# A new written-out order of instructions on all five queues of a fused linear-attention and feed-forward kernel

## The chip, the core and the metric

The kernel runs on one core of one Trainium2 chip. The core has a tensor engine (PE, TensorE), a vector engine (DVE), a scalar engine (ACT, ScalarE), GpSimd (POOL) and a sync engine (SP, SyncE) that mostly issues DMAs. Each engine works through its own list of instructions in order and waits on semaphores for the others. The metric is the device time of one execution, in microseconds (us).

## What is computed

Four batches, eight heads, 768 positions, head size 64. Block by block along the sequence, a decaying causal attention without softmax keeps a 64x64 state per head; its output x (3072 tokens x 512) goes through a feed-forward layer of width 2048 with the activation h + sin(alpha h)^2 / alpha.

```python
for b in range(nb):
    intra = np.einsum('bhic,bhjc->bhij', qb, kb) * Dmask[None]
    intra = np.einsum('bhij,bhjd->bhid', intra, vb)
    inter = np.einsum('bhid,bhde->bhie', qb * lam_pow[None], kv_state)
    out[:, :, sl] = intra + inter
    kv_state = lam_block[None, :, None, None] * kv_state + np.einsum('bhsd,bhse->bhde', kb_dec, vb)
...
h = x @ w_in
s = np.sin(alpha * h)
g = h + s * s / (alpha + 1e-09)
return (g @ w_out).astype(np.float32)
```

Inputs are float32; matmuls are in bfloat16 with float32 sums.

## The kernel before

**Attention in quads.** The attention is cut into 24 "quads" t = 0 to 23 (`quad0`, L758, for t below 8; `quad`, L959, for the others). For one quad: `ks`, `qs` multiply k and q by powers of lam and make them bfloat16 (L789 or L985; with .0 and .1 for halves), `vs` copies v to bfloat16 (L801, L804, L996). For t below 8, `Tk` and `Tq` transpose k and q on TensorE (L819) and `cT` copies the result out of PSUM (L825, L831); for t from 8 a DMA transposes (`DT`, L1008). `S` is the product of k and q (L850, L1021), `mask` the causal mask on it (L855, L1033, DVE), `Z` the state's increment (L867, L1072), `Zi` its copy for the second half of the quad (L886), `I` the part of the output from the state (L897, L1041), `O` the part from S and v (L912, L1061), `x` the copy of the result into the tile xT, which feeds the feed-forward part (L929, L1113); `Zs` (L952, L1136) and `Z` with a digit (L940, L1130) bring the state up to date. From t = 8 the S of the next quad stands in the same instruction group as O.

**Feed-forward in chunks.** Six chunks c of 512 tokens. `A c.m` (`grp_A`, L1146) makes 128 of the 2048 columns of h: 4 matmuls of 512 columns (L1160) into one of six PSUM banks. In chunk 0 some are made in halves of 256 tokens (h0, h1), two m at a time, as 8 matmuls of half width; a part of them with the first 2 or 3 of the 4 slices of x is a group of its own, marked e. Then `sin` (L1172, ACT), `sq`, the square (L1179 on ACT, L1180 on POOL or DVE) and `g` (L1184, DVE), which frees the bank. `B c.s.m` (`grp_B`, L1224) is 4 matmuls of the second product (L1237) for 128 tokens s and a quarter m of the 2048; after m = 3 the result is copied out (`o`, L1253) and stored (`st`, L1256). The last tile (`last_tile`, L1195) is made in three cuts (L1205, L1213, L1216).

**Loads.** The first eight quads' k, q, v come by `load_quad` (L746, tags `quad k0.1` and the like: the first digit counts pairs of heads, the second the half of the 256 rows of sequence; some loads take two pairs at once, 256 KB, others one, 128 KB). Quad 0 needs the pairs 0 and 1 with .0, quad 1 the pairs 2 and 3 with .0, quads 2 and 3 the same pairs with .1; quads 4 to 7 the numbers 4 to 7. One load, k1.0, is issued by ACT, the others by SyncE. The later quads' loads come by `load_half` (L635). The weights come in blocks w0, w0b (256 KB each in bfloat16), w1 to w7 (512 KB) through POOL's queue (`w_block`, L655). Small constants (`consts`, L675) are tagged c0 to c30: c12, c13 are the decay tables Lk, Lq of the quads 0 to 7, c15, c16 those of the others, c10 the logarithm of lam, c28 the loading of the sine table.

**What sets the order.** Every operation is recorded with the buffers that it reads and writes (`Program.add`, L220). `schedule` (L267) then lays the operations on the five engines. Where the table `ORDER` in `TUNE` gives a list for an engine, that list alone is the engine's order; dependencies become semaphore waits (`emit`, L458). What is left to `schedule`: which PSUM bank a group gets, and how many matmuls on zeros (`zero_mms`, L617, L619) stand in a gap that it expects on TensorE in the first 60 us; these fillers keep the engine active and are never read.

The lines that change are the five lists of `ORDER`, L59 to L158.

Of the kernel before, what the change touches and what calls it, by code (L numbers as in the profile page):

```python
# [58 lines left out]
    ORDER={'ACT': ['c0', 'alpha in', 'lam', 'c10', 'alpha', 'c13', 'c12', 'quad k1.0', 'c15', 'cT0.0', 'c16', 'vs1',  # L59
                   'cT1.0', 'x0', 'cT3', 'Zi1.0', 'c28', 'x1', 'Zs0.1', 'Zs1.1', 'Zs1.0', 'sin0.4h0', 'sin0.2h0',  # L60
                   'sin0.5h0', 'sq0.4h0', 'Zi3.0', 'x2', 'sin0.3h0', 'x3', 'sin0.1', 'sin0.4h1', 'sin0.5h1',
                   'sin0.8h1', 'sin0.9h1', 'sin0.8h0', 'sin0.0', 'sin0.9h0', 'sq0.0', 'sin0.6', 'sin0.7', 'sin0.11',
                   'sin0.2h1', 'sq0.11', 'sin0.3h1', 'vs4', 'sin0.13', 'sin0.12', 'sq0.12', 'sin0.14h0', 'sin0.14h1',
                   'sin0.15h0', 'sin0.15h1', 'sq0.14h1', 'cT4.1', 'oh1', 'vs7', 'vs5', 'Zi4.1', 'oh0', 'x4', 'vs6',
                   'Zi5.0', 'sin0.10', 'cT6', 'oh2', 'x5.0', 'Zi6.0', 'Zs4.0', 'Zs3.0', 'oh3', 'cT7', 'Zi7.1',
                   'sin1.1', 'sin1.3', 'sq1.3', 'sin1.0', 'sin1.2', 'sin1.6', 'sin1.4', 'sq1.6', 'sin1.5', 'Zs7.1',
                   'sq1.5', 'Zs7.0', 'sin1.7', 'vs9', 'sin1.9', 'sin1.11', 'sin1.8', 'sq1.8', 'sin1.10', 'sin1.13',
                   'Zs6.1', 'vs8', 'sin1.14', 'sq1.13', 'sin1.15', 'sq1.15', 'sin1.12', 'x8', 'Zs8.1', 'Zs8.0', 'x9',
                   'vs10', 'vs11', 'Zs9.0', 'Zs9.1', 'x10', 'x11', 'st0', 'o4', 'sin2.0', 'o5', 'sin2.3', 'sin2.1',
                   'sin2.4', 'sin2.2', 'st2', 'sin2.5', 'sin2.6', 'o6', 'sin2.8', 'sin2.11', 'sin2.7', 'st3', 'vs15',  # L70
# [12 lines left out]
                   'o22', 'st18', 'st22', 'o21', 'st20', 'st21', 'o23.0', 'st23.0', 'o23.2', 'st23.2'],
           'DVE': ['c24', 'c6', 'c1', 'c2', 'c19', 'c25', 'c8', 'c23', 'c22', 'c9', 'c11', 'qs0', 'c14', 'c18', 'ks3',
                   'vs0', 'ks0', 'qs1.1', 'cT0.1', 'cT1.1', 'Zi0.0', 'Zi0.1', 'c26', 'mask0', 'qs2.0', 'ks2.1',
                   'mask1', 'Zi1.1', 'Z0.0', 'Z0.1', 'cT2', 'c30', 'vs2', 'mask2', 'Zi2.0', 'Zs0.0', 'Zi2.1', 'Z1.1',
                   'mask3', 'Zi3.1', 'g0.5h0', 'g0.4h0', 'Z2.1', 'Z3.0', 'g0.2h0', 'Z3.1', 'cT4.0', 'sq0.4h1',
                   'g0.3h0', 'g0.4h1', 'g0.1', 'g0.5h1', 'g0.8h1', 'g0.0', 'qs5.1', 'g0.9h1', 'g0.8h0', 'g0.9h0',
                   'g0.7', 'g0.11', 'g0.6', 'sq0.13', 'g0.13', 'g0.2h1', 'g0.12', 'g0.3h1', 'g0.14h1', 'g0.15h1',
                   'g0.15h0', 'mask4', 'Zi4.0', 'cT5', 'g0.14h0', 'ks6.1', 'Z4.0', 'qs6.1', 'Z4.1', 'mask5', 'sq0.10',  # L90
                   'Zi5.1', 'g0.10', 'ks7.0', 'x5.1', 'qs7.0', 'Z5.0', 'Zi6.1', 'Zs4.1', 'mask6', 'Z5.1', 'Zs2.0',
                   'Zs5.1', 'x6', 'Z6.0', 'Zs2.1', 'Z6.1', 'Zs3.1', 'mask7', 'Zs5.0', 'Zi7.0', 'Zs6.0', 'o2', 'c21',
                   'x7', 'Z7.0', 'o3', 'Z7.1', 'g1.3', 'o0', 'sq1.0', 'sq1.1', 'g1.0', 'sq1.2', 'g1.1', 'g1.2', 'o1',
                   'g1.6', 'g1.5', 'g1.4', 'sq1.7', 'g1.7', 'g1.9', 'g1.8', 'sq1.10', 'g1.11', 'g1.10', 'g1.13',
# [12 lines left out]
                  'A0.11', 'A0.7', 'A0.2h1', 'B0.0.0', 'A0.13', 'A0.12', 'A0.14h0', 'A0.14h1', 'B0.1.0', 'B0.1.1',
                  'Tk4', 'B0.2.0', 'S4', 'Z4', 'Tk5', 'Tq5', 'B0.0.1', 'I4', 'O4', 'S5', 'Z5', 'A0.10', 'B0.3.0',
                  'Tk6', 'Tq6', 'B0.2.1', 'I5', 'O5', 'S6', 'Z6', 'B0.3.1', 'Tk7', 'Tq7', 'B0.2.2', 'I6', 'O6', 'Z7',
                  'S7', 'B0.1.2', 'B0.3.2', 'B0.2.3', 'B0.3.3', 'I7', 'O7', 'B0.0.2', 'A1.1', 'A1.3', 'A1.0',  # L110
                  'B0.0.3', 'A1.2', 'A1.6', 'A1.4', 'B0.1.3', 'A1.5', 'A1.9', 'A1.7', 'A1.11', 'A1.8', 'A1.10',
                  'A1.13', 'A1.14', 'A1.15', 'B1.0.0', 'B1.0.1', 'S8', 'A1.12', 'B1.0.2', 'O8', 'B1.1.0', 'B1.1.1',
                  'O9', 'B1.1.2', 'B1.0.3', 'O10', 'B1.1.3', 'B1.2.0', 'O11', 'B1.2.1', 'A2.0', 'A2.3', 'A2.1',
                  'A2.4', 'A2.2', 'A2.5', 'A2.6', 'B1.2.2', 'B1.2.3', 'A2.8', 'A2.11', 'A2.7', 'A2.12', 'A2.9',
                  'A2.10', 'B1.3.0', 'B1.3.1', 'B1.3.2', 'A2.13', 'B1.3.3', 'A2.15', 'A2.14', 'B2.0.0', 'O12',
                  'B2.0.1', 'B2.0.2', 'B2.1.0', 'O13', 'B2.1.1', 'B2.1.2', 'B2.2.0', 'O14', 'B2.0.3', 'B2.1.3', 'O15',
                  'B2.2.1', 'A3.1', 'A3.0', 'A3.2', 'A3.4', 'A3.7', 'A3.3', 'B2.2.2', 'A3.10', 'A3.5', 'B2.2.3',
                  'A3.6', 'A3.8', 'O16', 'B2.3.0', 'B2.3.1', 'B2.3.2', 'O17', 'A3.9', 'A3.11', 'A3.14', 'B2.3.3',
                  'A3.12', 'A3.15', 'O18', 'A3.13', 'B3.0.0', 'B3.0.1', 'O19', 'B3.0.2', 'A4.0', 'A4.1', 'B3.1.0',
# [1276 lines left out]
```

## Time and profile before

| what | value |
|---|---|
| runs shown | 215.23, 215.52, 216.65 us; median 215.52 |
| profiled execution | 216.6 us, its span 214.7 us |
| mean granted TensorE clock | 0.991 |
| busy: PE, DVE, ACT, POOL | 206.2, 126.1, 127.1, 125.8 us |
| matmuls on zeros (L619) | 110 of 2185, 9.5 us |
| HBM read, written | 27.27 MB, 6.29 MB |
| q, k, v loads of SyncE to landing, median of each kind | 4.2 to 10.3 us |

How to read the profile: a line of a timeline gives the start and the length in us, the engine, the line of the kernel, the operation, the tiles written and read, their shapes, the number of instructions merged, and in brackets how long the engine sat idle before and what released it. SPq, ACTq are the engines' issuing of DMAs; PEld is TensorE's weight load. A row of the table by stretches gives for each engine its busy time, then the granted TensorE clock, the mean busy share of the 16 DMA engines and GB/s. In the view of DMAs, q1 is SyncE's queue, q0 that of POOL, q10 that of ACT: packets, MB, and time taken as a share of the 16 engines in the stretch asked for; a row of issues gives KB each and the us from issue to landing.

### The profile page before, as it was taken

How to read it: one execution, taken by the hardware profiler on the slowest of the kernel's cores; microseconds unless marked ns; L12 is line 12 of the kernel's file. 1: busy time of each engine (PE TensorE's matmuls, PEld its weight loads, DVE VectorE, ACT ScalarE, POOL GpSimd, SP SyncE). 2: the span in 40 equal slices, each digit the busy share in tenths (PEclk: the TensorE clock that was granted, in tenths of full speed). 3: DMA queues.
4: the chain of work that ended last, by engine and by line, in shares of the span. 5: the costliest groups of instructions: out<-in, count | busy, mean ns of one | idle time of the engine just before them, and what ended most of it. 6: DMA issues, size and time to landing. Idle time of an engine off the chain costs nothing.

```text
span 214.7 us, 5310 instructions
## 1 busy us (share of the span) xinstructions
PE 206.2 (96%) x2185; PEld 110.7 (52%) x2185; DVE 126.1 (59%) x226; ACT 127.1 (59%) x236; POOL 125.8 (59%) x140
## 2 busy tenths in 40 slices
PE   7697899999999999999999999999999999999994
PEld 6684565655444455444455455454454544444454
DVE  4759578899868882454663477733616732463320
ACT  3056678975079955766536974957563726753231
POOL 2753387930328960799996988788765331771400
PEclk9998899999999999999999999999999999999999
DMA  5999999899998887999989999952630011310115
GB/s 154 281 215 226 216 262 267 206 173 185 181 202 163 174 151 164 231 219 223 222 115 228 198 244 172 191 125 84 101 98 0 3 49 52 147 62 35 52 52 194
DMA packets 88666, 33.91 MB, mean 158 GB/s; under 512 B 68402, under 2 KB 85698, under 8 KB 88642
## 3 DMA queue, kind: packets, MB, share of 16 engines
q1 hardware_dynamic: 79984, 23.01, 57.3%
q0 software_dynamic: 4752, 4.19, 12.3%
q10 hardware_dynamic: 3906, 6.37, 8.5%
q8 instruction: 17, 0.28, 0.6%
q14 instruction: 7, 0.06, 0.1%
HBM read 27.27 MB, written 6.29 MB: 156 GB/s over the span
## 4 chain that ended last, share of the span: by engine, by line
PE 87%; DMA 4%; SPq 3%; DVE 3%; ACT 2%; issue 1%; ACTq 0%
PE M_ps L1160 39%; PE M_ps L1237 37%; DMA q<-in_q_dram 4%; SPq L753 3%; PE M_ps L1061 2%; PE M_ps L1205 2%; PE M_ps L1041 2%; PE A_ps L1021 1%; DVE S_m L855 1%; PE M_ps L912 1%; PE M_ps L1072 1%; PE A_ps L850 1%; PE M_ps L819 1%; PE M_ps L867 1%; PE M_ps L897 1%
## 5 line engine op out<-in xcount | busy, mean ns | idle before, releaser
L1180 POOL TENSOR_TENSOR u<-t 128x512 bf16<-128x512 bf16 x73 | 74.6, 1039 | 51.0 <-ACT t L1172 50.1
L1184 DVE SCALAR_TENSOR_TENSOR gT<-u,r_sb,M_ps 128x512 bf16<-128x512 bf16 (+1 forms) x104 | 70.7, 703 | 56.5 <-POOL u L1180 51.7
L1160 PE MATMUL M_ps<-xT,w 128*128 128x512 bf16 (+1 forms) x416 | 90.4, 367 | 0.1
L1237 PE MATMUL M_ps<-w,gT 128*128 128x512 bf16 x368 | 87.8, 380 | 0.0
L1172 ACT ACTIVATE t<-M_ps,alpha_sb 128x512 bf16<-128x512 f32 (+1 forms) x104 | 65.5, 653 | 31.0 <-PE M_ps L1160 30.1
L1160 PEld LDWEIGHTS M_ps<-xT,w 128*128 128x128 bf16 x416 | 40.3, 99 | 43.1 <-DVE gT L1184 1.2
L1237 PEld LDWEIGHTS M_ps<-w,gT 128*128 128x128 bf16 x368 | 34.4, 98 | 39.4 <-DVE Zf L940 0.3
L985 POOL TENSOR_TENSOR qk<-k,Lk 128x512 bf16<-128x512 f32 x16 | 16.6, 1042 | 11.8 <-DMA k<-in_k_dram 11.8
L1113 ACT CAST xT<-M_ps 128x512 bf16<-128x512 f32 x16 | 9.3, 584 | 23.1 <-PE A_ps L1021 19.8
L1033 DVE TENSOR_TENSOR S_m<-A_ps,maskl 128x768 bf16<-128x768 f32 x16 | 15.3, 954 | 6.1 <-PE A_ps L1021 6.0
L985 POOL TENSOR_TENSOR qk<-q,Lq 128x512 bf16<-128x512 f32 x16 | 16.6, 1039 | 2.2 <-DMA q<-in_q_dram 1.8
L1253 ACT COPY osb<-M_ps 128x512 f32<-128x512 f32 x19 | 11.0, 585 | 10.5 <-PE M_ps L1237 10.3
L619 PE MATMUL M_ps<-zeros 128*128 128x128 bf16 (+1 forms) x110 | 9.5, 252 | 1.5 <-DVE zeros L679 1.5
L1136 ACT CAST Zq<-Zf 64x256 bf16<-64x256 f32 x24 | 9.7, 403 | 1.8 <-DVE Zf L1130 1.2
L855 DVE TENSOR_TENSOR S_m<-A_ps,maskq 128x1024 bf16<-128x1024 f32 x8 | 9.8, 1222 | 1.5 <-PE A_ps L850 1.4
L996 ACT CAST v<-v 128x512 bf16<-128x512 f32 x16 | 9.6, 618 | 1.1 <-DMA v<-in_v_dram 1.1
L619 PEld LDWEIGHTS M_ps<-zeros 128*128 128x128 bf16 x110 | 8.0, 114 | 1.7 <-DVE zeros L679 1.5
L789 POOL TENSOR_TENSOR qk<-q,Lq 128x256 bf16<-128x256 f32 (+1 forms) x7 | 5.2, 740 | 5.0 <-DVE qk L789 4.4
L819 PE MATMUL M_ps<-ident,qk 128*128 128x128 bf16 x64 | 5.2, 220 | 2.8 <-POOL qk L789 2.8
L1179 ACT ACTIVATE u<-t 128x512 bf16<-128x512 bf16 x11 | 6.9, 629 | 0.4
L1130 DVE TENSOR_TENSOR Zf<-M_ps,Zf 128x256 f32<-128x256 f32 x10 | 4.2, 418 | 4.3 <-ACT xT L1113 4.3
L789 POOL TENSOR_TENSOR qk<-k,Lk 128x512 bf16<-128x512 f32 (+1 forms) x6 | 4.9, 832 | 3.1 <-DMA k<-in_k_dram 2.5
(83 smaller groups left out, 136.5 us busy)
## 6 DMA issues: line engine op xcount, KB each, us to landing
q<-in_q_dram SPq DMA_DIRECT2D x23, 256.0 KB, 4.8
out_dram<-osb ACTq DMA_DIRECT2D x23, 256.0 KB, 2.3
v<-in_v_dram SPq DMA_DIRECT2D x38, 128.0 KB, 4.2
k<-in_k_dram SPq DMA_DIRECT2D x37, 128.0 KB, 4.6
w<-in_moe_w_out_dram POOLq DMA_DIRECT2D x4, 512.0 KB, 9.5
w<-in_moe_w_in_dram POOLq DMA_DIRECT2D x3, 512.0 KB, 11.3
k<-in_k_dram SPq DMA_DIRECT2D x5, 256.0 KB, 8.7
v<-in_v_dram SPq DMA_DIRECT2D x5, 256.0 KB, 10.3
```

The costliest lines, as they stand in the source:

```text
L619: last = e.matmul(m_ps[i][:, 0:c], zeros[:, 0:128], zeros[:, 0:c])
L789: rec(en, lambda e, L=L, gs=slice(g0, g0 + n): e.tensor_tensor(o[:, :, gs], i[:, :, gs], L, ALU.mult), *(((0.65, 0.58) if en == "DVE" else ...
L855: rec("DVE", lambda e: e.tensor_tensor(S_m[jm][:, :, :].rearrange("p (h a b) c -> p h a (b c)", h=2, a=2), Av().rearrange("p h (a x) -> p ...
L985: rec(en, lambda e, L=L, gs=slice(g0, g0 + m): e.tensor_tensor(o[:, :, gs], i[:, :, gs], L, ALU.mult), *(((0.65, 0.58) if en == "DVE" else ...
L1033: rec("DVE", lambda e: e.tensor_tensor(S_m[jm][:, :, :].rearrange("p (a b) c -> p a (b c)", a=4)[:, :, 0:192], A_ps[:, :, :].rearrange("p ...
L1136: rec(en, lambda e, rows=rows, en=en: (e.copy if en == "ACT" else e.tensor_copy)(Zq[jj][rows, :, rows], Zf[jj][rows, :, :].rearrange("p i ...
L1160: last = e.matmul(m_ps[vb.i][:, N * i:N * i + N], w1[:, kc, 128 * mm:128 * (mm + 1)], xT[x][:, kc, ts], start=(kc == 0 and i == 0), stop=( ...
L1172: rec("ACT", lambda e, i=i, mm=mm: e.activation(t16[tt][:, N * i:N * i + N], m_ps[vb.i][:, N * i:N * i + N], ACTF.Sin, scale=alpha_sb[:, m ...
L1180: return e.tensor_tensor(u16[tt][:, :], t16[tt][:, :], t16[tt][:, :], ALU.mult)
L1184: rec("DVE", lambda e, i=i, mm=mm: e.scalar_tensor_tensor(out=gT[g][:, mm, ts], in0=u16[tt][:, N * i:N * i + N], scalar=r_sb[:, mm:mm + 1] ...
L1237: last = e.matmul(m_ps[vb.i], gT[g][:, m, 128 * s4:128 * (s4 + 1)], w2[:, m, :], start=(m == 0 or (split and m == 8)), stop=(m == NM - 1 o ...
L1253: rec("ACT", lambda e: e.copy(osb[o][:, :], m_ps[vb.i]), 0.585, 0.48, reads=[vb.key], writes=[f"o.{o}"], frees=[vb], tag=f"o{gsi}")
```

## The change

All five lists of `ORDER` are replaced; nothing else in the file is touched. Each list has the same entries as before in another order: the search for the order was made anew with a set of delays in which every load lands late at random. The beginnings of the lists, which cover the first four quads:

```diff
-    ORDER={'ACT': ['c0', 'alpha in', 'lam', 'c10', 'alpha', 'c13', 'c12', 'quad k1.0', 'c15', 'cT0.0', 'c16', 'vs1',
-                   'cT1.0', 'x0', 'cT3', 'Zi1.0', 'c28', 'x1', 'Zs0.1', 'Zs1.1', 'Zs1.0', 'sin0.4h0', 'sin0.2h0',
+    ORDER={'ACT': ['lam', 'c0', 'c10', 'c16', 'alpha in', 'c12', 'c15', 'c13', 'quad k1.0', 'cT0.0', 'alpha', 'vs1',
+                   'Zi1.0', 'cT1.0', 'c28', 'x0', 'x1', 'cT3', 'Zs1.1', 'Zs0.1', 'Zs1.0', 'sin0.2h0', 'Zi3.0', 'x2',
...
-           'DVE': ['c24', 'c6', 'c1', 'c2', 'c19', 'c25', 'c8', 'c23', 'c22', 'c9', 'c11', 'qs0', 'c14', 'c18', 'ks3',
-                   'vs0', 'ks0', 'qs1.1', 'cT0.1', 'cT1.1', 'Zi0.0', 'Zi0.1', 'c26', 'mask0', 'qs2.0', 'ks2.1',
-                   'mask1', 'Zi1.1', 'Z0.0', 'Z0.1', 'cT2', 'c30', 'vs2', 'mask2', 'Zi2.0', 'Zs0.0', 'Zi2.1', 'Z1.1',
-                   'mask3', 'Zi3.1', 'g0.5h0', 'g0.4h0', 'Z2.1', 'Z3.0', 'g0.2h0', 'Z3.1', 'cT4.0', 'sq0.4h1',
+           'DVE': ['c2', 'c24', 'c8', 'c6', 'c22', 'c1', 'c26', 'c11', 'c23', 'c9', 'c19', 'c14', 'ks3', 'qs0', 'ks0',
+                   'vs0', 'ks2.1', 'cT0.1', 'qs1.1', 'cT1.1', 'c30', 'c18', 'c25', 'mask0', 'Zi0.0', 'vs2', 'Zi0.1',
+                   'qs2.0', 'mask1', 'Zi1.1', 'cT2', 'Z0.0', 'Z0.1', 'Zs0.0', 'Zi2.1', 'Zi2.0', 'mask2', 'Z1.1',
+                   'Zi3.1', 'mask3', 'Z2.1', 'Z3.0', 'g0.2h0', 'Z3.1', 'g0.4h0', 'g0.5h0', 'g0.3h0', 'sq0.4h1',
...
-           'PE': ['ln lam', 'alpha T', 'Tk1', 'Tk0', 'Tq0', 'Z0', 'S0', 'Tq1', 'I0', 'Tk3', 'Tq3', 'O0', 'S1', 'Z1',
-                  'A0.4h0e', 'Tk2', 'Tq2', 'I1', 'O1', 'S2', 'Z2', 'A0.4h0', 'A0.2h0e', 'A0.2h0', 'S3', 'I2', 'Z3',
-                  'O2', 'I3', 'O3', 'A0.4h1e', 'A0.1e', 'A0.1', 'A0.4h1', 'A0.8h1', 'Tq4', 'A0.8h0', 'A0.0', 'A0.6',
+           'PE': ['ln lam', 'Tq0', 'Tk0', 'Tk1', 'alpha T', 'Z0', 'S0', 'Tk3', 'Z1', 'Tq1', 'S1', 'I0', 'Tk2', 'Tq2',
+                  'O0', 'I1', 'O1', 'S2', 'Tq3', 'Z2', 'A0.2h0e', 'A0.2h0', 'I2', 'S3', 'Z3', 'O2', 'I3', 'A0.4h0e',
+                  'A0.4h0', 'O3', 'A0.1e', 'A0.4h1e', 'A0.1', 'A0.4h1', 'Tq4', 'A0.8h0', 'A0.0', 'A0.8h1', 'A0.6',
...
-           'POOL': ['c3', 'c17', 'c27', 'c20', 'c5', 'c4', 'qs2.1', 'c7', 'w1', 'w0b', 'ks1', 'c29', 'qs3', 'w0',
-                    'qs1.0', 'w2', 'ks2.0', 'w4', 'w3', 'vs3', 'sq0.2h0', 'qs4', 'sq0.1', 'w5', 'qs5.0', 'sq0.8h1',
+           'POOL': ['c3', 'c4', 'c5', 'ks1', 'w0b', 'c7', 'w0', 'c17', 'c27', 'w1', 'qs1.0', 'c29', 'ks2.0', 'qs2.1',
+                    'w2', 'w3', 'qs3', 'w4', 'vs3', 'sq0.2h0', 'qs4', 'w5', 'sq0.1', 'sq0.8h0', 'sq0.8h1', 'sq0.6',
...
-           'SP': ['quad q0.0', 'quad v0.0', 'quad q1.1', 'quad v1.0', 'quad v2.0', 'quad k2.1', 'quad k2.0',
-                  'quad k3.0', 'quad k0.0', 'quad q2.0', 'quad q2.1', 'quad k1.1', 'quad v3.0', 'quad q0.1',
-                  'quad k0.1', 'quad v0.1', 'quad v1.1', 'quad v2.1', 'quad q4.0', 'quad q6.0', 'quad v4.0',
+           'SP': ['quad k2.1', 'quad k3.0', 'quad v2.0', 'quad k2.0', 'quad k0.0', 'quad v1.0', 'quad q0.0',
+                  'quad v1.1', 'quad k0.1', 'quad v0.0', 'quad k1.1', 'quad q2.0', 'quad q0.1', 'quad v3.0',
+                  'quad q1.1', 'quad v0.1', 'quad q2.1', 'quad v2.1', 'quad q4.0', 'quad q6.0', 'quad k4.0',
```

Further on, in the lists behind these lines: POOL has qs14 and qs15 ahead of sq2.1, its first square of chunk 2 (before, behind ten squares of it); SyncE has the loads q7.1 and q7.0 directly behind DT12 and DT8 ahead of DT9; TensorE has the B groups of chunk 0 spread differently among the first A groups of chunk 1; ScalarE has cT3 behind x1 and x3 between sin0.4h0 and sin0.5h0. The built program has the same number of A, B and attention matmuls; the matmuls on zeros are 96 instead of 110, as 7, 74, 2, 2 and 7 of 128 columns and 3 and 1 of 512 (before 24, 45, 14, 9 and 16 of 128 columns and 1 and 1 of 512).

172 rows, old and new, of the table ORDER are left out of this document.

## The prediction

> **What bounds the kernel now.** I read the page first (busy time, slices, chain), then the chain in order of time, then the first 27 us instruction by instruction.
>
> ```profile
> span 214.7 us, 5310 instructions
> PE 206.2 (96%) x2185; PEld 110.7 (52%) x2185; DVE 126.1 (59%) x226; ACT 127.1 (59%) x236; POOL 125.8 (59%) x140
> ...
> PE   7697899999999999999999999999999999999994
> ...
> PE 87%; DMA 4%; SPq 3%; DVE 3%; ACT 2%; issue 1%; ACTq 0%
> ...
> L1180 POOL TENSOR_TENSOR u<-t 128x512 bf16<-128x512 bf16 x73 | 74.6, 1039 | 51.0 <-ACT t L1172 50.1
> L1184 DVE SCALAR_TENSOR_TENSOR gT<-u,r_sb,M_ps 128x512 bf16<-128x512 bf16 (+1 forms) x104 | 70.7, 703 | 56.5 <-POOL u L1180 51.7
> ...
> L1172 ACT ACTIVATE t<-M_ps,alpha_sb 128x512 bf16<-128x512 f32 (+1 forms) x104 | 65.5, 653 | 31.0 <-PE M_ps L1160 30.1
> ```
>
> TensorE is the bound: 96% busy, 87% of the chain, digits of 9 from the sixth slice to the last but one. What is not TensorE lies at the start. The chain in order of time:
>
> ```profile
> 7.88 7.95 DMA q<-in_q_dram
> ...
> 15.85 0.76 DVE qk L789 x2
> ...
> 26.11 2.72 PE M_ps L1160 x20
> ...
> 101.26 0.86 PE M_ps L1160 x4
> ...
> 135.97 0.63 ACT v L996
> ...
> 212.08 0.27 ACT osl L1213
> ```
>
> Until 15.85 the chain is SyncE's issue of loads and one load, q0.1; from 15.85 to 26.11 it alternates between vector, scalar and tensor work of the first four blocks ("quads" 0 to 3); from 26.11, where O3 has ended, to 212.08 it is matmul after matmul. I split the span there: start 26.1, TensorE's own stretch 212.08 - 26.11 = 186.0, tail 214.7 - 212.1 = 2.6. This execution took 216.6 us, 1.9 beyond its span, and lies 1.1 above the median of 215.52; the sum is made on 216.6 and then lowered by 1.1.
>
> **Part 1: the long stretch, same work in another order.** The number of A and B groups is unchanged, and only 96 zero matmuls replace 110, all of them before quad 3 is through. So the 186.0 can change only by waits. The only break that I found in it is the second of these lines:
>
> ```profile
> 87.39 2.10 POOL L1180 TENSOR_TENSOR u<-t 128x512 bf16<-128x512 bf16 x2 [8.72 <-ACT t L1172]
> ...
> 136.64 0.23 PEld L1041 LDWEIGHTS M_ps<-qkT,Zq 128*128 128x128 bf16 x4 [0.54 <-ACT v L996]
> ```
>
> It costs 0.54. There a copy of v stood behind an output copy on ScalarE. Where the order of after is tight I counted leads: between an A group and the first matmul that needs its result or its bank stand at least three groups of four matmuls and often four. The chain shows a group of four at 0.86, so four groups are 3.45, against sin 0.65, square 1.04, g 0.70 = 2.39 from the groups above. In both orders the shortest leads are alike (0.86 from x to the next A group at the head of each chunk, 3.45 for A to B); after drops one tight case in the first chunk (A0.7 to A0.12). On POOL qs14 and qs15 now stand ahead of the first square of chunk 2: 2 x 1.04, and their loads come right behind DT12 on SyncE; they lie in POOL's idle 8.72 before 87.39. If that cover were gone the squares, g and B1.3 would be late by up to 2.1. On SyncE the transposes stand at nearly the same amount of loads ahead of them (DT17 behind 10.0 instead of 9.9 MB, DT13 behind 6.0 instead of 7.1). v6 comes at 7.0 instead of 6.6 MB; v9 at 10.4 instead of 11.1. I take 0 for the stretch; bounds -0.5 (the break gone) and +2.1 (the POOL cover gone).
>
> **Part 2: the loads of the start.** SyncE issues the same 18 loads of the first four quads. Of those that were waited for, quad 2's q0.1 and k0.1 go from the 14th and 15th place to the 13th and 9th, its q1.1 from the 3rd to the 15th and v1.1 from the 17th to the 8th; v0.1 stays the 16th; quad 3's q2.1 goes from the 11th to the 17th. POOL issues w0b, w0, w1 instead of w1, w0b, w0.
>
> ```profile
> k<-in_k_dram SPq DMA_DIRECT2D x1, 128.0 KB, 8.1
> ```
>
> ```profile
> v<-in_v_dram SPq DMA_DIRECT2D x1, 128.0 KB, 8.9
> ```
>
> ```profile
> v<-in_v_dram SPq DMA_DIRECT2D x1, 128.0 KB, 9.5
> ```
>
> ```profile
> q0 software_dynamic: 182, 0.19, 112.2%
> q1 hardware_dynamic: 47, 0.02, 9.7%
> ```
>
> ```profile
> q0 software_dynamic: 195, 0.11, 75.8%
> q1 hardware_dynamic: 196, 0.09, 48.4%
> ```
>
> The first is k0.1, issued at 8.39: it ends the first 2432 KB of SyncE's loads at 16.5. The second is v0.1, the 16th load, issued at 8.90, at 17.8. The third is v1.1, issued at about 9.4, at 18.9, with which 2688 KB were in. In after v0.1 is again the 16th but ends 2432 KB, and q2.1 ends 2688 KB. The last two fences are the stretches 11 to 12 and 14 to 15 us: while w1 moves, SyncE's queue gets 0.02 MB per us, while w0b or w0 moves, 0.09. Because the small w blocks now go first, SyncE may be ahead by up to 1.3 us at that point: 15.2 at best, 16.5 for equal bytes, 17.8 for an equal slot. I take T = 16.2, near the row with the same bytes.
>
> **Part 3: from T to the end of O3.** DVE's order decides, since vs2 now stands ahead of Zi0.1, qs2.0 and mask1.
>
> ```profile
> 4.99 0.41 ACTq L753 DMA_DIRECT2D k<-in_k_dram  x1
> ...
> 12.90 1.23 DVE L855 TENSOR_TENSOR S_m<-A_ps,maskq 128x1024 bf16<-128x1024 f32 x1
> ...
> 15.85 0.43 DVE L789 TENSOR_TENSOR qk<-q,Lq 128x256 bf16<-128x256 f32 x1 [1.73 <-DMA q<-in_q_dram]
> ...
> 16.53 1.22 DVE L855 TENSOR_TENSOR S_m<-A_ps,maskq 128x1024 bf16<-128x1024 f32 x1
> ...
> 17.76 0.29 DVE L886 CAST Zi<-M_ps 64x128 bf16<-64x128 f32 x1
> ...
> 18.62 0.69 DVE L825 COPY qkT<-M_ps 128x1024 bf16<-128x1024 bf16 x1
> ...
> 18.88 0.39 PE L619 MATMUL M_ps<-zeros 128*128 128x512 bf16 x1
> ...
> 19.36 0.43 PE L850 MATMUL A_ps<-qkT 64*64 64x128 bf16 x16
> 19.38 0.36 DVE L804 CAST v<-v 128x512 bf16<-128x512 f32 x1
> 19.80 0.42 PE L867 MATMUL M_ps<-v,qk 64*64 64x64 bf16 x8
> 19.83 1.22 DVE L855 TENSOR_TENSOR S_m<-A_ps,maskq 128x1024 bf16<-128x1024 f32 x1
> ...
> 20.16 2.74 PE L1160 MATMUL M_ps<-xT,w 128*128 128x256 bf16 x12
> ...
> 22.83 0.50 PE L850 MATMUL A_ps<-qkT 64*64 64x128 bf16 x16
> ...
> 25.70 0.42 PE L912 MATMUL M_ps<-S_m,v 64*64 64x128 bf16 x16
> ```
>
> Ahead of T: ScalarE now computes the tables of the later quads and issues alpha before the tables that the first need; so load k1.0, issued at 4.99 before (first row), goes out at about 5.7 (an estimate: the first of those tables waits for 0.7 of small vector pieces) and quad 0 starts some 0.7 later. That is hidden: DVE reaches its wait for v0.1 at about 15.2 (mask0 ended at 12.90 + 1.23 = 14.1, plus 0.7, plus Zi0.0 0.3), still ahead of T. If T were 15.2, this would be what is late next.
>
> From T on: vs2 0.36, Zi0.1 0.29, qs2.0 0.43, mask1 1.22, Zi1.1 0.29, cT2 0.69: 3.28, so cT2 ends at 19.5; before it ended at 18.62 + 0.69 = 19.3. S2 0.43 to 19.95. Now Tq3 stands here (half of quad 3's transposes, taken as 0.4 like S2 and Z2; its q2.1 lands, by equal bytes, at 18.9, and POOL, at 1.04 like its squares, has it scaled by 20.0) to 20.4, Z2 0.42 to 20.8. DVE: Zi2 twice, 0.6, and mask2 1.22 to 22.6; before, mask2 ended at 19.83 + 1.22 = 21.05. Meanwhile TensorE does 8 half-width matmuls of A0.2 instead of 12: at 2.74 / 12 each that is 1.83, to 22.6, and a filler 0.39 to 22.95. I2 0.5, S3 0.43, Z3 0.3, to 24.2; Zi3.1 0.29 and mask3 1.22 to 25.75; I3 and the 8 matmuls of A0.4h0 (0.5 and, at full clock, 0.9 as for four of full width) fit beside mask3 after O2, to 26.0; O3 0.42 to 26.4. By then as many A matmuls (16) are done as before at 26.1. So the start is longer by **+0.3**: the 1.4 lost on mask2 is nearly given back, since S3 in before came only at 22.83, behind 12 slow matmuls.
>
> Sum: 216.6 + 0.3 + 0 = 216.9 for a run like the profiled one, 215.5 + 0.3 = **215.8** against the median.
>
> **The clock in that stretch** is the part that the durations above hang on:
>
> ```profile
> 16.00:17.00 1.00, 0.34 (x4) 0.05 (x1) 1.00 (x3) 0.98 (x3) 0.41 (x1) 1.00 1.24 274
> ...
> 19.00:20.00 1.00, 0.90 (x25) 0.46 (x24) 0.91 (x4) 0.95 (x3) 0.00 (x0) 0.82 1.27 220
> 20.00:21.00 1.00, 1.00 (x13) 0.69 (x10) 1.00 (x2) 0.43 (x2) 0.00 (x0) 0.50 1.21 217
> ...
> 23.00:24.00 1.00, 1.00 (x50) 0.81 (x50) 0.62 (x1) 0.97 (x3) 0.00 (x0) 0.97 1.19 210
> ```
>
> The granted clock (third number from the end) falls to 0.50 from about 19.65 to 23.0, after a stretch in which TensorE had little to do (0.34 busy from 16 to 17), and the 12 matmuls cost about twice. I assumed the same for A0.2h0 in after.
>
> **The rivals.**
> (a) Faster. v0.1 at 15.2 (-1.0) and no half clock: A0.2h0 then takes 0.9, S3 starts at mask2's end and O3 ends 1.2 sooner; with the break at 136.6 gone (-0.5) 215.8 - 2.7 = 213.1. For it: w0b and w0 leave SyncE 0.09 per us. Against: less filler stands between 9 and 20 us.
> (b) Slower: vs2 blocks DVE. With T = 17.8, as the 16th load landed before, everything in part 3 moves by 1.6: 217.4. It decides from T = 18.1 on (over 1%). For it: before, DVE waited for q0.1, which only quad 2's scaling needs, while Zi0 and mask0 were long done; now quad 0's Zi0.1 waits too. Against: 128 KB less lies ahead of it.
> (c) Slower: the half clock lasts over A0.4h0 and the first full groups: 0.9 there, 0.4 on S3, Z3 and I3: 217.0. The Trainium skill, "TensorE: Matmul & The Clock Gate", section "What's actually happening", says that the clock is granted by TensorE's activity in free-running windows of some 3.4 us; the fall of about 3.4 us in the rows agrees. By that rule a sparser start can lose a second window, which is this rival.
> (d) The long stretch does not keep up and gains a wait as in part 1: 215.8 + 2.1 = 217.9.
>
> **How the numbers follow.** Forecast 0.57, (a) 0.14, (b) 0.13, (c) 0.09, (d) 0.07. I forecast the first, 215.8, whose own range is 214.3 to 217.0 (T 15.2 to 16.9, clock as before). The range reaches to (a) and beyond (b) with half of (c): 213.4 to 218.3. About 1% (2.2 us) is what a measurement of this kernel can tell from no change. Faster by over 1%: most of (a), 0.13. Slower by over 1%: (d), most of (b) with a bit of (c) on top, and a tail of the forecast: 0.25. Within: 0.62.
>
> **What would show it.** In after: vs2 (L804 on DVE) starting at 16.2 behind a DMA wait; cT2 ending near 19.5; mask2 ending near 22.6; L912 of O3 ending near 26.4; the granted clock at 0.50 for one window, not two; TensorE's own stretch at 186 +- 0.5. The forecast is wrong if that wait ends after 17.5, if the clock is low beyond 24, or if a TensorE wait over 1 us stands behind 30 us.

## The result, and the profile after

After takes 224.81 us (median of 4 runs, 223.89 to 225.43), before took 215.76 in the runs beside it (215.23 to 216.65). The ratio is 1.0412, 95% interval 1.0359 to 1.0464: 9 us slower. The forecast was 215.8, with 213.4 to 218.3 as its range. Ratios here leave disturbed executions out; medians are over all runs, so where they differ the ratio counts.

The profiled execution of after took 223.89 us. From its page, the span, the busy times, the slices of TensorE and of its clock, and the chain:

```profile
span 222.0 us, 5256 instructions
PE 204.3 (92%) x2140; PEld 110.5 (50%) x2171; DVE 134.4 (61%) x226; ACT 126.3 (57%) x236; POOL 127.0 (57%) x140
...
PE   6959999999999269999999999999999999999995
...
PEclk9988999999999859999999999999999999999999
...
PE 78%; DVE 9%; ACT 4%; SPq 3%; DMA 3%; issue 3%; ACTq 0%
```

Where before had nines from the sixth slice to the last but one, there are now a 2 and a 6 (slices 14 and 15, 72 to 83 us), and right there the clock reads 8 and 5. DVE has 9% of the chain, up from 3. (TensorE's 92% is a little too low: 2140 matmuls are recorded for 2171 weight loads, so some short gaps called "issue" are lost records.)

The chain in order of time goes straight to the place:

```profile
70.80 1.32 DVE gT L1184 x2
72.12 0.03 issue
72.15 6.88 DVE maskl L722
79.03 0.03 issue
79.06 0.76 DVE gT L1184
79.82 0.05 issue
79.86 4.43 PE M_ps L1237 x12
```

One DVE instruction of 6.88 us: c21, the copy of the causal mask maskl from rows 0 to 63 to rows 64 to 127. It is the same instruction in before. The first row is its group in after's page, the second is from before's DVE timeline, the third from before's POOL timeline:

```profile
L722 DVE COPY maskl<-maskl 64x192 bf16<-64x192 bf16 x1 | 6.9, 6881 | 0.0
```

```profile
56.32 0.20 DVE L722 COPY maskl<-maskl 64x192 bf16<-64x192 bf16 x1
```

```profile
57.30 2.04 POOL L985 TENSOR_TENSOR qk<-k,Lk 128x512 bf16<-128x512 f32 x2 [11.75 <-DMA k<-in_k_dram]
```

In before it stood behind o2 at 56.32 us, while POOL idled (11.75 us before 57.30). In after it stands behind g1.10, and what it reads, POOL's fill c20 (an affine select, L717: it sets the elements of a tile that meet a condition on row and column), has moved from the start of POOL's list to a place between ks10 and sq1.12. POOL's timeline in after:

```profile
70.48 1.23 POOL L985 TENSOR_TENSOR qk<-k,Lk 128x512 bf16<-128x512 f32 x1
71.66 0.30 POOL L717 TENSOR_SCALAR_AFFINE_SELECT maskl<-zeros 64x128 bf16<-64x128 bf16 x1
71.92 2.04 POOL L1180 TENSOR_TENSOR u<-t 128x512 bf16<-128x512 bf16 x2
73.92 1.04 POOL L985 TENSOR_TENSOR qk<-q,Lq 128x512 bf16<-128x512 f32 x1
...
77.92 1.05 POOL L985 TENSOR_TENSOR qk<-q,Lq 128x512 bf16<-128x512 f32 x1
91.58 2.04 POOL L985 TENSOR_TENSOR qk<-q,Lq 128x512 bf16<-128x512 f32 x2 [12.62 <-DMA q<-in_q_dram]
```

Seven instructions follow the fill without a gap (such a series is called POOL's row below), and the copy ends at 79.03, 0.06 after the last of them (77.92 + 1.05 = 78.97). Then, on TensorE:

```profile
72.44 1.03 PE L1237 MATMUL M_ps<-w,gT 128*128 128x512 bf16 x4
79.86 4.43 PE L1237 MATMUL M_ps<-w,gT 128*128 128x512 bf16 x12 [6.40 <-DVE gT L1184]
```

g1.11 is queued right behind the copy, and the next group, B1.0.0, writes into the PSUM bank that g1.11 has to free. TensorE waits 6.40 us, and the 12 matmuls behind the wait take 4.43 (0.37 each, where a group of four takes 0.86 elsewhere in the chain, 0.22 each). The granted clock (third number from the end) shows why: it stays at half until 83.26, over the first 3.4 us of this work:

```profile
79.00:80.00 1.00, 0.14 (x1) 0.13 (x2) 0.97 (x3) 0.00 (x0) 0.00 (x0) 0.50 0.00 0
80.00:81.00 1.00, 1.00 (x3) 0.30 (x2) 1.00 (x2) 0.00 (x0) 0.00 (x0) 0.50 0.00 0
...
82.00:83.00 1.00, 1.00 (x4) 0.43 (x3) 1.00 (x2) 0.00 (x0) 0.00 (x0) 0.50 0.00 0
83.00:84.00 1.00, 1.00 (x6) 0.39 (x4) 0.30 (x1) 0.00 (x0) 0.00 (x0) 0.87 0.08 16
```

Measured as the prediction measured it, from the end of O3 to the last output copy, the long stretch in after comes from these two rows:

```profile
24.96 0.42 PE L912 MATMUL M_ps<-S_m,v 64*64 64x128 bf16 x16
```

```profile
219.70 0.27 ACT osl L1213
```

219.70 - 25.38 = 194.3, against 186.0 in before: +8.3. The start ended at 25.38 instead of 26.12: -0.7. Together +7.6, and the spans differ by 222.0 - 214.7 = 7.3; the rest of 0.3 lies in the tail, 2.3 after the last output copy's start instead of 2.6.

### The profile page after: what moved, and what is told of

Same layout as the page of the kernel before. It is cut to its first block, busy times and chain, and to the rows that moved or that the text cites. A ratio compares the mean times of both kernels' runs of the same rounds, so it can differ in the third digit from the quotient of the medians.

```text
span 222.0 us, 5256 instructions
## 1 busy us (share of the span) xinstructions
PE 204.3 (92%) x2140; PEld 110.5 (50%) x2171; DVE 134.4 (61%) x226; ACT 126.3 (57%) x236; POOL 127.0 (57%) x140
## 4 chain that ended last, share of the span: by engine, by line
PE 78%; DVE 9%; ACT 4%; SPq 3%; DMA 3%; issue 3%; ACTq 0%
PE M_ps L1160 34%; PE M_ps L1237 33%; DVE maskl L722 3%; SPq L753 3%; DMA v<-in_v_dram 3%; DVE gT L1184 2%; PE M_ps L1061 2%; PE M_ps L1205 2%; PE M_ps L1041 1%; ACT t L1172 1%; PE A_ps L1021 1%; DVE S_m L855 1%; PE M_ps L897 1%; DVE qk L789 1%; PE M_ps L912 1%
## 5 line engine op out<-in xcount | busy, mean ns | idle before, releaser
L1237 PE MATMUL M_ps<-w,gT 128*128 128x512 bf16 x351 | 86.1, 385 | 8.4 <-DVE gT L1184 6.4
L1160 PE MATMUL M_ps<-xT,w 128*128 128x512 bf16 (+1 forms) x404 | 87.9, 362 | 1.3 <-issue 1.0
L1160 PEld LDWEIGHTS M_ps<-xT,w 128*128 128x128 bf16 x416 | 39.4, 98 | 42.3 <-DVE gT L1184 2.3
L1237 PEld LDWEIGHTS M_ps<-w,gT 128*128 128x128 bf16 x368 | 34.9, 99 | 47.8 <-DVE gT L1184 7.3
L1180 DVE TENSOR_TENSOR u<-t 128x512 bf16<-128x512 bf16 x12 | 6.6, 552 | 4.4 <-ACT t L1172 4.3
L722 DVE COPY maskl<-maskl 64x192 bf16<-64x192 bf16 x1 | 6.9, 6881 | 0.0
```

The lines of the kernel that those rows point to most:

```text
L722: rec("DVE", lambda e: e.tensor_copy(maskl[64:128, :], maskl[0:64, :]), 0.15, reads=["maskl"], writes=["maskl"])
L1160: last = e.matmul(m_ps[vb.i][:, N * i:N * i + N], w1[:, kc, 128 * mm:128 * (mm + 1)], xT[x][:, kc, ts], start=(kc == 0 and i == 0), stop=( ...
L1180: return e.tensor_tensor(u16[tt][:, :], t16[tt][:, :], t16[tt][:, :], ALU.mult)
L1237: last = e.matmul(m_ps[vb.i], gT[g][:, m, 128 * s4:128 * (s4 + 1)], w2[:, m, :], start=(m == 0 or (split and m == 8)), stop=(m == NM - 1 o ...
```

## The experiments

Theory 1: the loss is the long copy and what follows from it (the wait, then the clock). Rival, theory 2: the rest of the new order loses by itself. SyncE's transposes DT11 and DT12 stand 11.40 us from 74.99, and POOL then idles 12.62 for q7, which could be a second cost or a mere consequence, since DT12 needs O8 behind the late B1. Once the copy's place was confirmed, the question became what makes it long.

**e1 and e12: fill and copy back into POOL's idle time.** The same kernel twice, with 10 executions and with 12.

```diff
 POOL
-  'ks10', 'c20', 'sq1.12'
+  'qs7.1', 'c20', 'sq1.4'
 DVE
-  'g1.10', 'c21', 'g1.11'
+  'mask7', 'c21', 'x6'
```

> The order of after, with the two pieces that make maskl moved back into the time in which POOL idles: POOL's fill (c20) behind qs7.1, DVE's copy (c21) behind mask7. Theory 1, the copy is held up by POOL's row of work, and all of the loss is its 6.88 us, the 6.4 us for which TensorE waits behind it, and the slow clock that follows: the copy takes about 0.2 us, TensorE's wait before B1 is gone, and the time falls from 224.8 to 214.5 to 216 (the start of after is 0.7 us shorter than that of before, 215.8 less 0.7 is 215.1). Theory 2, the new order of loads, transposes and POOL's scalings costs by itself (two transposes stand 11.4 us on SyncE from 74.99, POOL then idles 12.62 for q7): the squares of chunk 2 still come at about 93 and the time stays over 218.

> The order of after with fill and copy of maskl in POOL's long idle time, timed in more rounds. Theory 1, the long copy is all that the new order lost and the rest of the order is worth what the prediction had for it (+0.3 in the start, 0 beyond): 215.5 to 216.5, a ratio to before of 0.998 to 1.004. Theory 2, its start is really shorter, as the profiled run of after had it (0.7): 214.5 to 215.3, a ratio of 0.994 to 0.998.

Measured: the copy 0.20 us, no wait of TensorE before B1; e1 at a ratio of 0.9959 (0.9911 to 1.0006) and a median of 215.77 against 216.16, e12 at 0.9978 (0.9943 to 1.0014), 216.25 against 216.15. Theory 1 of e1 holds and its theory 2 falls: the 8.3 us are gone, and no loss by the order's other moves is left that these intervals could tell. Between the two theories of e12 the interval does not decide. From e12's rows:

```profile
26.12 0.42 PE L912 MATMUL M_ps<-S_m,v 64*64 64x128 bf16 x16
```

```profile
212.05 0.27 ACT osl L1213
```

212.05 - 26.54 = 185.5 for the long stretch, and a start that here is 0.4 longer than that of before.

**e4: only the fill back, the copy left behind g1.10.**

```diff
 POOL
-  'ks10', 'c20', 'sq1.12'
+  'qs7.1', 'c20', 'sq1.4'
```

> The order of after, with POOL's fill of maskl (c20) moved forward behind qs7.1, and DVE's copy (c21) left behind g1.10. It tells whether the copy is long because what it reads comes late or because of its own place. Theory 1, its place beside POOL's unbroken row: no change, the copy takes 6 to 7 us and the time is 223.5 to 225. Theory 2, it waits for c20: 0.2 us and 214.5 to 216.

Measured: 216.73 against 216.16, ratio 1.0029 (0.9987 to 1.0071). This was a miss for theory 1 as I had put it (any copy beside POOL's unbroken row lasts until the row ends). Theory 2 missed too, by less: the copy took 0.61 us and not 0.2, and the time lies 0.7 above its range. The DVE row, and POOL's row at that time:

```profile
73.29 0.61 DVE L722 COPY maskl<-maskl 64x192 bf16<-64x192 bf16 x1
```

```profile
72.80 2.03 POOL L1180 TENSOR_TENSOR u<-t 128x512 bf16<-128x512 bf16 x2
74.80 1.04 POOL L985 TENSOR_TENSOR qk<-q,Lq 128x512 bf16<-128x512 f32 x1
```

The copy waits for the first of the two squares to end (72.80 + about 1.03 = 73.83) and ends at 73.90: it gets its turn between two POOL instructions that follow without a gap.

**e2: before, with the copy alone moved behind g1.10.**

```diff
 DVE
-  'o2', 'c21', 'x7'
+  'g1.10', 'c21', 'g1.13'
```

> The order of before, with one instruction moved: the copy of maskl (c21) goes from behind o2 to behind g1.10 on DVE; POOL's fill c20 stays at the start. Theory 1, a plain DVE copy that starts while POOL works without a gap lasts until that row ends: POOL's row of qs12, qs11, sq1.14, ks12, sq1.12, ks13 runs from 72.63 to 78.66, the copy would start at about 73.8 and take some 4.9 us instead of 0.20, g1.13 and mask8 would come some 4.6 us late, and the time is 218 to 222 against 215.8. Theory 2: the place of the copy costs nothing, 215.5 to 216.

Measured: the copy 0.92 us, median 217.66 against 216.16, ratio 1.0030 (0.9983 to 1.0078). Here, too, it slipped in at the end of one POOL instruction. So the copy's place costs up to one POOL instruction and not 4.9 us; theory 1 missed again, and the median lies below its range and above that of theory 2.

**e3: after, with nothing moved, but the copy marked so that POOL waits for it.**

```diff
-                writes=["maskl"])
+                writes=["maskl"], port="whole")
```

> The order of after, nothing moved, but the copy of maskl is recorded with the port mark that the squares and scalings of DVE have, by which a POOL instruction that follows is made to wait for it; here that is qs11, after sq1.12 and sq1.14. Theory 1, the copy lasts until POOL pauses: it ends with sq1.14, 2.1 us after its start instead of 6.88, TensorE's wait before B1 shrinks from 6.4 to about 1.6, and the time is 216 to 217.5. Theory 2, the copy is slow by itself at this place or waits for something else: still 6 to 7 us and 223 to 225.

The copy's row:

```profile
72.10 1.88 DVE L722 COPY maskl<-maskl 64x192 bf16<-64x192 bf16 x1
```

Measured: the copy 1.88 us, TensorE's wait 1.4, ratio 1.0070 (1.0025 to 1.0116), median 217.74, 0.2 above the range. The clock stayed at 1.00 in every microsecond from 72 to 84: a wait of 1.4 did not lower it. The copy missed the boundary between sq1.12 and sq1.14 and got in only where POOL stopped for it, near the 2.1 expected.

What differs between after and e3 on one side and e4 and e2 on the other? The fill stands in POOL's row, the copy carries a wait for POOL's semaphore, and the copy reads what was just written. Three theories, and a fourth: one chip's moment.

**e5: after itself once more, beside e6 to e8.**

> The kernel after itself, unchanged, on the chip of the runs beside it: the copy of maskl that only lost its late fill took 0.61 us and not 6 to 7, so it must be known whether the 6.88 us come back on another chip. Theory 1, the long copy belongs to the order: 6.8 to 6.9 us again, 223 to 226 us. Theory 2, it was one chip's or one moment's: 0.6 to 2 us, 215 to 218.

Measured: the copy 6.87 us, TensorE's wait 6.4, 224.13 against 215.60, ratio 1.0392 (1.0338 to 1.0446). It belongs to the order.

**e6 and e7: who carries the wait.** e6 adds a wait to the copy of e4; e7 takes it from the copy of after.

```diff
 e6, on e4
+            at = {o.tag: o for o in P.ops}
+            at["c21"].deps.add(at["ks10"])
             P.emit(nc, sem)
 e7, on after
+            rec("DVE", lambda e: e.memset(junkd[:, :], 0.0), 0.1, after=[P.ops[-1]], tag="wait20")
             rec("DVE", lambda e: e.tensor_copy(maskl[64:128, :], maskl[0:64, :]), 0.15, reads=["maskl"],
 DVE
-  'g1.10', 'c21', 'g1.11'
+  'g1.10', 'wait20', 'c21', 'g1.11'
```

> POOL's fill c20 early, and the copy left behind g1.10, where it took 0.61 us; now the copy is also made to wait for ks10, POOL's last piece before the two squares, which is done by then, so that the copy carries a wait for POOL's semaphore as it does in after. Theory W, a copy that itself carries such a wait misses POOL's turns until POOL pauses: 6 to 7 us, 222 to 225 us. Theory F, the fill in the midst of POOL's row is what matters: 0.6 us, 215.5 to 217.5.

> The order of after, with one tiny DVE memset put ahead of the copy to carry its wait for POOL's fill; the copy itself then carries none, and starts some 0.1 us later against POOL's squares. Theory W, the wait on the copy matters: the copy gets in when the first square ends, 0.5 to 0.9 us, 215.5 to 217.5. Theory F, the fill in POOL's row matters: 6 to 7 us and 222 to 225. If the memset itself is held for microseconds, both are wrong and the place in time is what decides.

Measured: e6 0.62 us for the copy, ratio 0.9989 (0.9951 to 1.0026); e7 0.06 us for the memset and 6.86 for the copy, ratio 1.0478 (1.0427 to 1.0528). The wait on the copy does not matter; theory W falls, F stands. The time of e7, 226.17, is above F's range all the same: in its profiled execution the clock was at 0.50 from 12.3 to 26 us and over 4.7 us of the work behind the wait, against 3.4 in after.

**e8: after, with the copy one place later, behind g1.11.**

> The order of after, with the copy one place later on DVE, behind g1.11, its wait for the fill kept. It becomes ready about 0.66 us later, at 0.9 of the first square's 1.04. Theory W: still until POOL's row ends, 6.2 us, but B1 can start with g1.11; g1.12 is late, 221 to 225. Theory P, the instant at which the copy comes within POOL's instruction decides: it gets in within 0.2 to 1.2 us, and the time is 215 to 217.5.

Measured: the copy 6.21 us, from 72.7 to the end of POOL's row again; TensorE now waits 5.4 for mask8 behind it; ratio 1.0346 (1.0271 to 1.0420). The instant within POOL's instruction is not what decides.

**e9 and e10: the fill as data, or as an instruction.** On e4, where the copy took 0.61, one more POOL instruction into a tile that nobody reads is put at the fill's late place: in e9 the same affine select, in e10 an iota.

```diff
 e9, POOL
-  'ks10', 'sq1.12'
+  'ks10', 'fill2', 'sq1.12'
 e10, POOL
-  'ks10', 'sq1.12'
+  'ks10', 'iota2', 'sq1.12'
```

> POOL's fill of maskl early and the copy behind g1.10, as where it took 0.61 us; in addition POOL makes a second fill of the same shape, into a tile that nobody reads, at the late place of the first, between ks10 and sq1.12. Theory F, a fill (affine select) in the midst of POOL's row takes DVE's turns away until the row ends, whatever it writes: the copy 6 to 7 us, 223 to 226 us. Theory D, what counts is that the copy reads what POOL has just written: 0.6 us, 215.5 to 217.5.

> As the run with the second fill, but the extra POOL instruction between ks10 and sq1.12 is an iota of 128 partitions into a tile that nobody reads. If any POOL instruction that is no tensor operation between two tensors does it: the copy 6 to 7 us and 223 to 226. If it is the fill alone: 0.6 us and 215.5 to 217.5.

Measured: e9 1.0351 (1.0290 to 1.0412), e10 0.9991 (0.9956 to 1.0027). The groups of e9, and then of e10:

```profile
L728 DVE COPY maskl<-maskl 64x192 bf16<-64x192 bf16 x1 | 6.9, 6864 | 0.0
...
L723 POOL TENSOR_SCALAR_AFFINE_SELECT spare<-zeros 64x128 bf16<-64x128 bf16 x1 | 0.3, 286 | 0.0
```

```profile
L725 DVE COPY maskl<-maskl 64x192 bf16<-64x192 bf16 x1 | 0.7, 710 | 0.0
...
L723 POOL IOTA spare<- 128x6 int32 x1 | 0.1, 129 | 0.0
```

This is the clearest pair: a fill whose result nobody reads brings the whole loss back, an iota in its place does not. (The iota is also smaller and reads no tile; which of these differences counts is not shown.)

**e11: the fill two places earlier, with a pause of POOL behind it.**

```diff
 POOL
-  'sq1.9', 'sq1.11', 'ks10', 'c20', 'sq1.12'
+  'sq1.9', 'c20', 'sq1.11', 'ks10', 'sq1.12'
```

> The order of after with POOL's fill two places earlier, behind sq1.9, where POOL then waits about 1.5 us for ScalarE before sq1.11; the copy stays behind g1.10. Theory F, the effect of the fill ends with POOL's next pause: the copy gets in after one square, 0.6 us, 215.5 to 217.5. If a fill within some 4 us is enough: 6 to 7 us and 223 to 225.

Measured: the copy 0.61, ratio 0.9998 (0.9957 to 1.0039). From POOL's row, and the copy:

```profile
68.09 0.48 POOL L717 TENSOR_SCALAR_AFFINE_SELECT maskl<-zeros 64x128 bf16<-64x128 bf16 x1
69.63 1.04 POOL L1180 TENSOR_TENSOR u<-t 128x512 bf16<-128x512 bf16 x1 [1.06 <-ACT t L1172]
```

```profile
72.30 0.61 DVE L722 COPY maskl<-maskl 64x192 bf16<-64x192 bf16 x1
```

Here the fill has no effect: the copy came 4.2 us after its start and had its turn. That fits theory F, by which the pause of 1.06 us ends the effect. But two other things changed with it: a DVE square got a turn between the pause and the copy (ks10 behind it took 1.22), and the copy came later after the fill than in the runs in which it was held (at most 1.7 us, e15). The run does not separate them from the pause.

**e13: the copy on ScalarE, the fill left in the row.**

```diff
-            rec("DVE", lambda e: e.tensor_copy(maskl[64:128, :], maskl[0:64, :]), 0.15, reads=["maskl"],
+            rec("ACT", lambda e: e.copy(maskl[64:128, :], maskl[0:64, :]), 0.3, reads=["maskl"],
 ACT
+  'sin1.14', 'c21', 'st0'
 DVE
-  'g1.10', 'c21', 'g1.11'
+  'g1.10', 'g1.11'
```

> The order of after with POOL's fill left in its row, but the copy of maskl made by ScalarE, behind sin1.14, instead of DVE. Theory 1, only DVE is locked out by POOL's row: the copy takes under 0.5 us, TensorE's wait before B1 is gone, 215 to 217. Theory 2, whatever reads maskl then is held, or the fill itself is late: ScalarE stands for some 6 us, and the time stays over 221.

Measured: 0.35 us on ScalarE, no wait before B1, ratio 0.9985 (0.9943 to 1.0027). ScalarE is not held by the row that holds DVE's copy.

**e14: TensorE kept busy during the wait.** 28 zero matmuls before B1.1.0, in after's order, with the long copy left as it is.

```diff
+            wb = P.bank()
+            rec_pe(lambda e: zero_mms(e, 28, wb.i, 512), [(FULL, 0.0)], ["zeros"], [wb.key], claim=wb,
+                   frees=[wb], prio=0, tag="keep")
             P.emit(nc, sem)
 PE
-  'A1.13', 'B1.1.0'
+  'A1.13', 'keep', 'B1.1.0'
```

> The order of after with the long copy left as it is, and 28 zero matmuls of 512 columns (28 x 0.2157 = 6.04 us) on TensorE before B1.1.0, in the time in which it waits for the copy. Theory 1, what the loss has beyond the wait of 6.4 is the clock of 0.50 that follows it: the clock stays at 1.00 behind the wait, the 12 matmuls behind it take 2.6 us instead of 4.43, and the time is 222 to 222.8 (1.7 to 1.8 less than after). Theory 2, the lowered clock is not tied to TensorE's idleness: still 0.50 for some 3.4 us, 223.5 to 225.

Measured: the copy 6.87, ratio 1.0263 (1.0200 to 1.0326), below the interval of after (1.0359 to 1.0464), median 222.32. TensorE's timeline and the granted clock:

```profile
72.58 6.21 PE L619 MATMUL M_ps<-zeros 128*128 128x512 bf16 x28
78.62 1.03 PE L1237 MATMUL M_ps<-w,gT 128*128 128x512 bf16 x4
80.00 2.76 PE L1237 MATMUL M_ps<-w,gT 128*128 128x512 bf16 x12 [0.35 <-DVE gT L1184]
```

```profile
80.00:81.00 1.00, 1.00 (x5) 0.50 (x6) 1.00 (x2) 0.00 (x0) 0.00 (x0) 1.00 0.00 0
```

The clock is 1.00 where it was 0.50, and the same 12 matmuls take 2.76 instead of 4.43. That is the second term of the loss: 4.43 - 2.76 = 1.7. The whole stretch is 217.61 - 25.53 = 192.1, 2.2 shorter than in after.

**e15: a fill ahead of a DVE square.** The kernel of e9 with its second fill moved in front of ks10, executed once.

```diff
 POOL
-  'sq1.11', 'ks10', 'fill2', 'sq1.12'
+  'sq1.11', 'fill2', 'ks10', 'sq1.12'
```

> The copy early enough not to read a late fill, and a second fill of a tile that nobody reads in POOL's row between sq1.11 and ks10, while DVE's square sq1.10 waits for its turn (without a fill it gets in at the end of sq1.11, 0.85 us, and ks10 takes 1.22 instead of 1.04). Theory A, a fill locks out DVE's squares as well: sq1.10 takes about 1.1 us more, until ks10 has ended and POOL itself waits for it. Theory B, copies alone: 0.85 us again.

Measured: the square took 0.85 as ever, but that does not show squares to be exempt; the execution took 224.93 us. On DVE and on POOL:

```profile
71.08 0.85 DVE L1186 TENSOR_TENSOR u<-t 128x512 bf16<-128x512 bf16 x1 [0.23 <-ACT t L1178]
...
73.28 6.87 DVE L728 COPY maskl<-maskl 64x192 bf16<-64x192 bf16 x1
```

```profile
70.61 1.04 POOL L1186 TENSOR_TENSOR u<-t 128x512 bf16<-128x512 bf16 x1 [1.49 <-ACT t L1178]
71.60 0.48 POOL L723 TENSOR_SCALAR_AFFINE_SELECT spare<-zeros 64x128 bf16<-64x128 bf16 x1
72.06 1.04 POOL L991 TENSOR_TENSOR qk<-k,Lk 128x512 bf16<-128x512 f32 x1
73.06 2.04 POOL L1186 TENSOR_TENSOR u<-t 128x512 bf16<-128x512 bf16 x2
```

The square got in at the boundary ahead of the fill, and the fill, not ks10, was the one that waited (0.48 instead of 0.29). So the run does not tell whether squares are locked out behind a fill; that stays open. What it does show is that a whole POOL instruction between the fill and the copy's coming (ks10; sq1.12 had begun) does not help: the copy is again held until the row ends, 6.87 us.

## Why the prediction was wrong, point by point

**Part 1, the long stretch: this step failed.** It said that the 186.0 "can change only by waits" and took 0, with +2.1 as the upper bound. The first half is right for 6.4 of the 8.3 (it left out that a wait can slow the matmuls behind it, which made 1.7); the bound was built from one place only. I counted leads with durations from before (sin 0.65, square 1.04, g 0.70), as if a duration moved with its instruction. The copy c21 (0.20 us) and its fill c20 (0.3) do not appear in the working at all: the change of their place was put at nothing without a reason. The copy's duration depends on what POOL does beside it, and the pair went from POOL's idle time into POOL's busiest row. With the two put elsewhere the stretch is 185.5 (e12), and with a copy that is not held it is, in e11 and e13, 212.28 - 25.52 = 186.8 and 211.50 - 25.37 = 186.1: the 0 was right, within 0.8, for all that I had counted.

The loss of the stretch, 8.3, splits into the wait of 6.4 (shown by e12, e4, e9) and 1.7 of half clock behind it (shown by e14); 0.2 is left over. The 1.7 is that of one execution: the same 12 matmuls took 4.18 us in e5 and 4.98 in e9.

**The POOL cover, qs14 and qs15 ahead of chunk 2's squares**, which had the +2.1: it held. In e3 the order is the same and only the long copy is cut:

```profile
84.90 2.04 POOL L985 TENSOR_TENSOR qk<-q,Lq 128x512 bf16<-128x512 f32 x2 [5.81 <-DMA q<-in_q_dram]
89.61 2.04 POOL L1180 TENSOR_TENSOR u<-t 128x512 bf16<-128x512 bf16 x2 [2.67 <-ACT t L1172]
```

POOL has done both and then still waits 2.67 for ScalarE. The 12.62 in after and the 11.40 on SyncE came for the most part from the late O8: in e13, without the long copy, they are 5.31 and 3.41.

**The break of 0.54 at 136.64** is gone, as the bound of -0.5 had it (in after's chain behind 90 us nothing but TensorE's work stands, with pieces of "issue" of at most 0.16), but the stretch did not get shorter by it: 185.5 to 186.8 in e4, e6 and e10 to e13 against 186.0.

**Part 2, T.** The row of vs2 in after:

```profile
15.01 0.58 DVE L804 CAST v<-v 128x512 bf16<-128x512 f32 x1 [0.33 <-DMA v<-in_v_dram]
```

T is 15.0, where 16.2 was taken and 15.2 was the best case. The loads were ahead of both bounds; that the small w blocks first did it fits, but no run shows it.

**Part 3.** cT2 ended at 18.65 + 0.69 = 19.34 (forecast 19.5), mask2 at 21.02 + 1.21 = 22.23 (22.6), O3 at 25.38 (26.4):

```profile
18.65 0.69 DVE L825 COPY qkT<-M_ps 128x1024 bf16<-128x1024 bf16 x1 [0.73 <-PE M_ps L819]
...
21.02 1.21 DVE L855 TENSOR_TENSOR S_m<-A_ps,maskq 128x1024 bf16<-128x1024 f32 x1
```

T came 1.2 earlier and cT2 only 0.2: vs2 took 0.58 instead of 0.36 (why is not shown; POOL was issuing a load of the weights), and cT2 waited 0.73 for its transposes. The half clock came once, as forecast, but from 15 to some 18.4 us, ahead of A0.2h0 and not over it, so those 8 matmuls took 1.03 and not 1.83; they were done at 21.45 instead of 22.6, TensorE then waited 0.52 for ScalarE, and O3 came 1.0 early. Rival (c) did not happen. The +0.3 was within what one execution can tell: in e4, e6 and e10 to e13, kernels with the same start, O3 ends at 24.23 (e10) to 26.54 (e12).

**The rivals.** (d), a wait in the long stretch, was the one that happened. It had 0.07 and a price of 2.1, for another place and another cause. The sentence that a TensorE wait over 1 us behind 30 us would refute the forecast named the right thing to look for.

**Why POOL's row holds a DVE copy.** The runs show a turn at the next boundary between two POOL instructions (e4, e2, e6, e10, e11: 0.61 to 0.92 us, ending where a POOL instruction ends). They show none for a copy that comes behind an affine select, once the next instruction of the row has started, until POOL pauses (after, e3, e5, e7, e8, e9, e14, e15). The Trainium skill, "SBUF — State Buffer", section "Who interferes with whom", says that DVE in a two-port mode and GpSimd exclude each other on a shared pair of ports, the first to issue holding it for its whole instruction. The runs without a fill in the row agree with that: the copy waits for one POOL instruction. By that rule after's copy would have waited for one POOL instruction, up to 1.04; it took 6.88, so the measurement decides: behind the fill DVE's copy is held over all the instructions that are left in the row. Whether it is this pair of ports that is kept, and why, is not shown.

At the fill's own end a turn is possible. At the start of e13 a DVE scaling came while POOL made another affine select, until about 10.0, and the affine select behind that one was held up (it takes 0.19 us in before):

```profile
9.68 0.90 DVE L789 TENSOR_TENSOR qk<-k,Lk 128x512 bf16<-128x512 f32 x1 [0.97 <-DMA k<-in_k_dram]
```

```profile
9.98 0.66 POOL L728 TENSOR_SCALAR_AFFINE_SELECT identf<-maskf 16x16 f32<-16x16 f32 x1
```

Whether a copy that waits there gets in as well, no run shows. The planner of this kernel could not see the loss either: the copy is recorded without the mark that makes it model the pair, and its model gives the pair back after every instruction.

**The clock.** The prediction counted the half clock at the start only. The place where it mattered was here: 6.4 us of idleness cost another 1.7, 1.4 us of idleness (e3) cost nothing more. By the rows of after, e5, e7 and e9 the clock was at 0.50 for 6.8 us each time, from a point within the wait on; how much of it falls on work (2.9 us in e5, 4.7 in e7) depends on when it begins.

## What to carry to other kernels

A duration read from a trace belongs to an instruction and its neighbours: when a reordering moves a DVE copy, look up what POOL does at the new time, however short the copy was before. Keep one-time set-up (fills, mask copies) out of POOL's unbroken rows, give it to ScalarE, or let POOL wait for it; each of the three won the 9 us back, the last all but some 1.5 of them. A kernel that keeps TensorE busy pays for a long wait twice, once for the wait and once for the clock behind it.

## What the runs showed of the hardware that was not expected

- Behind an affine select of 64x128 (0.29 us) in POOL's row, a DVE copy of 64x192 that came behind the fill's end got no turn until POOL paused: 1.88, 6.21 and 6.86 to 6.88 us, always ending 0.06 or 0.07 after the last instruction before the pause. Without the fill the copy took 0.61 to 0.92 beside such a row. An iota (0.13 us) in its place had no such effect (0.71), and a fill with a pause of 1.06 us behind it had none (0.61). Other fills and other DVE operations were not told apart.
- DVE's g (one operand in SBUF, one in PSUM) was never held: about 0.74 beside POOL's row in these runs. ScalarE's copy of the same mask took 0.35 beside it.
- When DVE does get its turn, POOL pays: ks10 behind the square took 1.22 instead of 1.04.
- TensorE's clock stayed at 1.00 in a wait of 1.4 us. In waits of 6.4 us it fell to 0.50 for 6.8 us, of which 2.9 to 4.7 us lay on the work behind the wait.
